# Conversions of later weight blocks queued behind the last routing, product groups placed between routing steps, and a second result buffer

## The chip, the cores and the metric

The kernel runs on one core of one Trainium2 chip. The metric is the time of one execution on the device in microseconds (us); the figure given for a kernel is the median of its runs. A profile is one more execution, with every instruction recorded.

A core has five engines, each with its own queue that is worked through in the order in which the program was written out: TensorE (PE in the profile, its weight loads are PEld), VectorE (DVE), ScalarE (ACT), GpSimd (POOL) and SyncE (SP), which here only starts transfers.

## The reference

Three stages follow one another.

```python
# 1. a linear attention with a complex decay, per batch and head
S_re, S_im = ar*S_re - ai*S_im + k v^T, ar*S_im + ai*S_re
y[t] = q[t] @ S_re
# 2. a mixture of 8 experts, one expert for each token
expert_idx = np.argmax(x @ w_gate, axis=1)
out[mask] = gate_w[mask] * (np.maximum(xe @ w1[e], 0) @ w2[e])
# 3. a dense part
h = (x @ w1) * (x @ w2) @ w3
return h @ w_out
```

There are 3072 tokens of 384 numbers; the inner width of the experts and of the dense part is 1024. The weights of the dense part come as 64-bit floating point numbers.

## The kernel before

**Folding.** `w3 @ w_out` does not depend on the tokens. The kernel computes this 1024 x 384 matrix once (class `Fuse`, L670), writes it to device memory as `wf`, and later needs one product per token instead of two. The matrix has eight row blocks `f` of 128. `Fuse.product` (L707) makes a block with 24 matmuls into one PSUM bank: eight column tiles `g`, three matmuls each (`mm3`, L349, a split into a high and a low part). It yields after every second `g`, so a product is issued in four groups of six matmuls. Then ACT copies the bank to a buffer `ws` (L722), and SP stores `ws` to `wf` (L723). In the trace the first six products are named `Wf`, the last two `wpo`.

**Conversions.** Each block needs its weights as a high and a low 32-bit part, `w3h` and `w3l`. `Fuse._singles` (L681) generates these steps through `halves` (L313): eight units for `w_out`, then two for each of the eight blocks, "half blocks" below. A unit is spread over three successive steps: a first stage on DVE (L336, L337, L339) on the raw numbers `fdr` that SP has loaded, a stage on ACT (L329, L330), a second stage on DVE (L322, L323, L324) that writes `w3h` and `w3l`. There are five raw buffers, and `ahead` asks for loads up to two units ahead of the one in hand. The blocks' results lie in four sets of buffers; block `f` takes the set of block `f - 4`, so its second stage must wait until product `f - 4` has read it.

**Routing.** `route` (L110) takes two finished token tiles: transposes on PE (L122, `rt`), a copy by ACT (`xt`, L124), logits on PE (L131, `rl`), a copy by ACT (`lg`, L132), a chain of small DVE steps (maximum `mx`, L137; `key`; `kx`; one-hot `oh`, L144), ranks on PE (L147 to L150, `rk`), three DVE steps to the positions `pi` (L152 to L156), and on POOL an indirect transfer per tile (L160) that scatters its rows to the buffers of the experts, `xs`.

**Experts.** `moe` (L442) loads an expert's 432 rows of `xs` as `xe` (L385), transposes them (L395, `px`), splits them into `xh` and `xl`, and runs eight steps per expert. A step is `hstep` (L399): nine matmuls `ph`, a relu by ACT (`hh`, L406), a remainder by DVE (`hl`, L407); and `ystep`, nine matmuls `py`. After each `hstep` the loop asks the generator of the products for one more piece (L492), so the last two products and their conversions come here, one piece per step; when they are used up, the conversion of the other dense weights begins (`moe2_weights`, L506).

**What sets the order.** The program is traced in the order of the Python code, and a scheduler then writes out a queue for each engine. It prefers what was traced earlier, but puts in later work where it reckons that an engine would stand idle. `tc.issue_after(ins)` adds a constraint: what is traced in that block stays behind `ins` on the engine of `ins`, and only on that engine. Before the change all conversions are held behind `S.end` alone (L702), the last DVE step of attention's keys, so those of blocks 4 to 7 may be put in anywhere after it. Four blocks are asked for during the last group of attention (L1132). The loop in `build` (L1332) then issues products until six blocks are done, all of it behind `x.lasty`, attention's last output matmul. The conversions of blocks 4 and 5 are traced in this loop, those of 6 and 7 in the expert steps.

Of the kernel before, what the change touches and what calls it, by code (L numbers as in the profile page):

```python
# [1 line left out]

# [6 lines left out]
F32 = mybir.dt.float32  # L9
# [11 lines left out]
DM = 384  # L21
KD = 3
NE = 8
FF = 1024
NF = 8
# [71 lines left out]
def bc(ap, n, at):  # L97
    shape = list(ap.shape)
    return ap.unsqueeze(at).to_broadcast(shape[:at] + [n] + shape[at:])
# [10 lines left out]
def route(tc, S, slot0, xtiles, bank=None):  # L110

    nc = tc.nc
    n = len(xtiles)
    sp = S.rpool
    bank = bank or (lambda name: S.rpsum.tile([128, 512], F32, tag="tr", name=name, bufs=2))
    slots = slice(slot0, slot0 + n)
    lg, mx = S.lg[:, slots], S.mx[:, slots]
    xts = []
    for i, x in enumerate(xtiles):
        pt = bank(f"rt{slot0}_{i}")[:, : KD * 128].rearrange("p (k c) -> p k c", k=KD)  # L120
        for k in range(KD):
            nc.tensor.transpose(pt[:, k], x[:, k * 128 : (k + 1) * 128], S.ident)  # L122
        xts.append(sp.tile([128, KD, 128], F32, tag="xt", name=f"xt{slot0}_{i}", bufs=2))
        nc.scalar.copy(xts[-1], pt)  # L124
        yield 330
        if i % 2:
            yield None
            pl = bank(f"rl{slot0}_{i}")
            for j, xt in enumerate(xts):
                for k in range(KD):  # L130
                    nc.tensor.matmul(pl[:, j * NE : (j + 1) * NE], xt[:, k], S.wg[:, k], start=(k == 0), stop=(k == KD - 1))  # L131
            S.logits = nc.scalar.copy(lg[:, i - 1 : i + 1].rearrange("p i e -> p (i e)"), pl[:, : 2 * NE])  # L132
            xts = []
            yield 1280
    t8 = lambda nm: sp.tile([128, n, NE], F32, tag=nm, name=f"{nm}{slot0}")
    v = nc.vector
    v.reduce_max(out=mx[:, :, 0], in_=lg, axis=AX.X)  # L137
    key = t8("key")
    for i in range(n):
        v.scalar_tensor_tensor(out=key[:, i], in0=lg[:, i], scalar=mx[:, i], in1=S.efirst, op0=ALU.is_ge, op1=ALU.mult)  # L140
    kx = sp.tile([128, n, 1], F32, tag="kx", name=f"kx{slot0}")
    v.reduce_max(out=kx[:, :, 0], in_=key, axis=AX.X)
    oh = t8("oh")
    v.tensor_tensor(out=oh, in0=key, in1=kx.to_broadcast([128, n, NE]), op=ALU.is_equal)  # L144
    yield None
    rk = bank(f"rk{slot0}")[:, : n * NE].rearrange("p (i e) -> p i e", e=NE)
    nc.tensor.matmul(rk, S.ones, bc(S.run, n, 1), start=True, stop=False)  # L147
    nc.tensor.matmul(rk, S.upper, oh, start=False, stop=n == 1)
    for i in range(1, n):
        nc.tensor.matmul(rk[:, i:], S.ones, bc(oh[:, i - 1], n - i, 1), start=False, stop=i == n - 1)  # L150
    r2 = t8("r2")
    v.tensor_tensor(out=r2, in0=rk, in1=oh, op=ALU.mult)  # L152
    pos = S.pos[:, slots]
    v.reduce_sum(out=pos, in_=r2, axis=AX.X)
    pi = sp.tile([128, n], I32, tag="pi", name=f"pi{slot0}")
    S.routed = v.tensor_copy(pi, pos)  # L156
    for i in range(n):
        v.tensor_tensor(out=S.run, in0=S.run, in1=oh[:, i], op=ALU.add)
    for i, x in enumerate(xtiles):
        S.scatter = nc.gpsimd.indirect_dma_start(  # L160
            out=S.xsv[slot0 + i], out_offset=bass.IndirectOffsetOnAxis(ap=pi[:, i : i + 1], axis=0),
            in_=x, in_offset=None, bounds_check=NE * CAPR - 1, oob_is_err=False,
        )
    yield 640
# [113 lines left out]
def ahead(load, srcs, n):  # L278

    got = []  # L280
    for i in range(len(srcs)):
        while len(got) < min(i + n, len(srcs)):
            got.append(load(srcs[len(got)]))
        yield got[i]
# [155 lines left out]


def moe(tc, S, fuse, product):  # L442

    nc = tc.nc
    extra = moe2_weights(tc, S)
    with ExitStack() as pools:
        pool = lambda n, bufs, **kw: pools.enter_context(tc.tile_pool(name=n, bufs=bufs, **kw))
        steps = [(e, j) for e in range(NE) for j in range(NF)]
        LA, LR = 1, 4
        x = Expert(tc, S, pool("mw", 3), None, None, S.rpsum, None)  # L450
        ws, xs, xraw = {}, {}, {}
        wraw = {i: x.load_w(*steps[i], nc.sync) for i in range(LR)}
        yield
        x.xp, x.hp, x.py = pool("mx", 2), pool("mh", 2), pool("mpy", 1, space=PSUM)
        fuse.psum = lambda f, name: x.py.tile([128, 512], F32, tag="px", name=name, bufs=KD)
        xraw[0] = x.load_x(0, nc.sync)
        def weights(i):
            with tc.issue_after(S.routed.ins), tc.issue_after(S.logits.ins):
                ws[i] = x.split_w(*wraw.pop(i))

        for i in range(LA):
            weights(i)
        xs[0] = x.make_xt(xraw[0])
        pend = None
        psy = None

        def flush():
            nonlocal psy
            i, h = pend
            e, j = steps[i]  # L470
            if j == 0:
                psy = x.py.tile([128, KD, 512], F32, tag="py", name="py")
            x.ystep(psy, h, ws[i], j)
            if j == NF - 1:
                x.store(psy, nc.scalar.value_load(S.offi[0:1, e : e + 1], min_val=0, max_val=NT))
            del ws[i]

        for i, (e, j) in enumerate(steps):
            if i + LR < len(steps):
                wraw[i + LR] = x.load_w(*steps[i + LR], nc.sync)  # L480
            if i + LA < len(steps):
                weights(i + LA)
            if j == 1 and e < NE - 1:
                with tc.issue_after(x.relu.ins):
                    xraw[e + 1] = x.load_x((e + 1) * CAPR, nc.scalar)
            h = x.hstep(xs[e], ws[i])
            if i == REND or (e, j) == (NE - 1, NF - 3):
                yield
            if pend is not None:
                flush()  # L490
            pend = (i, h)
            if next(product, None) is None:  # L492
                next(extra, None)
            if j == 5 and e + 1 < NE:
                with tc.issue_after(x.mark.ins):
                    xs[e + 1] = x.make_xt(xraw[e + 1])
            if j % 4 == 3 and i > NF:
                with tc.issue_after(x.late.ins):
                    next(S.places, None)
        flush()  # L500
        for x in (product, extra):
            for _ in x:
                pass
# [166 lines left out]
class Fuse:  # L670
# [10 lines left out]
    def _singles(self):  # L681
        nc, S, wp = self.nc, self.S, self.wp
        self.wo = [wp.tile([128, NF, DM], F32R, tag=f"wo{x}", name=f"wo{x}") for x in "hl"]
        self.w3 = []

        def factor(f):
            return lambda: [x[:, f] for x in self.wo]

        def block(f, h):
            def place():  # L690
                if not h:
                    pool = wp if f % W3B == 0 else self.w2p
                    self.w3.append([pool.tile([128, NF, 128], F32R, tag=f"w3{x}{f % W3B}", name=f"w3{x}{f}") for x in "hl"])
                return [x.rearrange("p g c -> p (g c)")[:, h * 512 : (h + 1) * 512] for x in self.w3[f]]
            return place

        srcs = [S.w_out[f * 128 : (f + 1) * 128, :] for f in range(NF)]
        srcs += [S.w3[f, :, h * 512 : (h + 1) * 512] for f in range(NF) for h in range(2)]
        raws = ahead(doubles(self.w2p, nc.sync, 5), srcs, 3)
        made = halves(S, nc, raws, wp, [factor(f) for f in range(NF)] + [block(f, h) for f in range(NF) for h in range(2)])  # L700
        for n in range(len(srcs) + 2):
            with self.tc.issue_after(S.end.ins):  # L702
                next(made)
            self.ready = max((n - 1 - NF) // 2, 0)
            yield

    def product(self):  # L707
        nc = self.nc
        for f in range(NF):
# [5 lines left out]
            for g in range(NF):  # L715
                mm3(nc, po[:, :DM], wh[:, g], wl[:, g], self.wo[0][:, g], self.wo[1][:, g], g == 0, g == NF - 1)
                if g % 2 and g < NF - 1:
                    if self.ready < min(f + W3B, BEFORE):
                        next(self.units)
                    yield 960  # L720
            ws = self.w2p.tile([128, DM], F32, tag="ws", name=f"ws_{f}")
            nc.scalar.copy(ws, po[:, :DM])  # L722
            nc.sync.dma_start(self.S.wf[f * 128 : (f + 1) * 128, :], ws)  # L723
            self.blocks = f + 1
# [558 lines left out]
BEFORE = 6  # L1283
W3B = 4


def build(ctx, tc, S):
    nc = tc.nc
# [7 lines left out]
    with ExitStack() as at:  # L1296
# [6 lines left out]
        x = Attn(tc, S, *(p.__enter__() for p in (qp, e2, ep)), st, pp, ap)  # L1303
# [25 lines left out]
            yield from x.groups(lambda *a: route(tc, S, *a), side, lambda: done)  # L1329

        drive([first(), second()])
        while side.fuse.blocks < BEFORE:  # L1332
            with tc.issue_after(x.lasty.ins):
                next(side.product)
    S.late = lambda name: ctx.enter_context(tc.tile_pool(name=name, bufs=1, side="right"))
    psum = tc.tile_pool(name="ph", bufs=2, space=PSUM)
# [59 lines left out]
```

## Time and profile before

| | |
|---|---|
| median of 3 runs | 1015.89 us (1015.53 to 1018.94) |
| the profiled execution, its own time | 1012.96 us |
| its span in the profile | 1011.2 us |
| PE busy | 896.7 us (89% of the span) |
| DVE busy | 610.1 us (60%) |
| ACT busy | 488.8 us (48%) |
| POOL busy | 126.8 us (13%) |

Times in the trace count from the start of the span. A matmul's start is its own; its end is modelled and overlaps the next one, so starts are compared below. A line of the timeline gives the start, the duration (of all instructions merged in it), the engine, the line, what it writes and reads, how many instructions are merged, and in brackets the idle time of the engine before it with what ended it. The granted clock of TensorE is given as a share of its full speed.

### The profile page before, as it was taken

What the parts mean: (1) busy time and instruction counts of PE and PEld (TensorE: products, weight loads), DVE (VectorE), ACT (ScalarE), POOL (GpSimd) and SP (SyncE); (2) the same over time, 40 slices, a digit from 0 to 9 for tenths busy, and PEclk for the clock granted to TensorE, in tenths of its full rate; (3) what the DMA queues carried; (4) which work ended last, traced back from release to release, by engine and by line L of the source; (5) the groups of instructions that cost most, each with busy time, mean ns of one, the idle gap of its engine ahead of it and who ended that gap; (6) DMA issues with size and microseconds to landing.
All of it is one profiled execution on the core that took longest, in us unless ns stands there. A gap on an engine that the chain in (4) does not pass through costs nothing. (4 is left out here: it accounts for less than half of the span.)

```text
span 1011.2 us, 17058 instructions
## 1 busy us (share of the span) xinstructions
PE 896.7 (89%) x6402; PEld 762.8 (75%) x6402; DVE 610.1 (60%) x1374; ACT 488.8 (48%) x1089; POOL 126.8 (13%) x197
## 2 busy tenths in 40 slices
PE   3544899968897899969989999998999999999997
PEld 1222478655786787969978999997888888888886
DVE  6899899797996797545379996443232323232222
ACT  6455588764874786424355665453222222121211
POOL 5111000102010101000222221110001010101011
PEclk9666899989998999979999999999999999999999
DMA  5556985339544973544585765550000000000000
GB/s 188 178 177 197 293 264 180 127 110 346 167 162 132 345 241 104 164 124 131 127 267 163 190 155 131 141 92 2 1 1 32 1 32 1 32 1 32 2 30 31
DMA packets 90183, 128.74 MB, mean 127 GB/s; under 512 B 7233, under 2 KB 72689, under 8 KB 90097
## 3 DMA queue, kind: packets, MB, share of 16 engines
q1 hardware_dynamic: 76300, 82.61, 29.0%
q0 software_dynamic: 10688, 40.36, 11.3%
q10 hardware_dynamic: 3108, 4.65, 1.8%
q8 instruction: 51, 0.84, 0.3%
q14 instruction: 36, 0.29, 0.1%
HBM read 92.38 MB, written 35.22 MB: 126 GB/s over the span
## 5 line engine op out<-in xcount | busy, mean ns | idle before, releaser
L605 DVE TENSOR_TENSOR ab<-asb,pb 128x512 f32<-128x512 f32 x48 | 33.0, 688 | 188.2 <-PE pb L352 184.9
L346 DVE TENSOR_TENSOR l<-w,h 128x384 fp32r<-128x384 f32 x128 | 70.8, 556 | 70.4 <-ACT h L345 64.3
L345 ACT CAST h<-w 128x384 fp32r<-128x384 f32 x128 | 65.4, 514 | 98.2 <-PE ph L351 50.5
L600 ACT COPY asb<-pa 128x512 f32<-128x512 f32 x48 | 28.2, 586 | 121.1 <-PE pa L352 117.2
L804 PE MATMUL x<-s,ident 128*128 128x384 f32 x64 | 35.6, 692 | 48.6 <-ACT s L856 48.4
L345 ACT CAST gh<-ab 128x512 fp32r<-128x512 f32 x48 | 29.8, 620 | 95.2 <-DVE ab L605 90.7
L351 PE MATMUL py<-hl,h 128*128 128x432 f32 x192 | 70.4, 367 | 2.9 <-DVE hl L407 2.8
L350 PE MATMUL py<-hh,h 128*128 128x432 f32 x192 | 69.7, 363 | 2.8 <-ACT hh L406 2.8
L350 PE MATMUL ph<-xh,h 128*128 128x432 f32 x192 | 69.9, 366 | 0.2 <-DVE hl L407 0.2
L352 PE MATMUL ph<-xh,l 128*128 128x432 f32 x192 | 69.6, 363 | 0.0
L351 PE MATMUL ph<-xl,h 128*128 128x432 f32 x192 | 69.4, 361 | 0.0
L352 PE MATMUL py<-hh,l 128*128 128x432 f32 x192 | 69.3, 361 | 0.0
L848 DVE TENSOR_TENSOR pr<-cf,P 128x192 f32<-128x192 f32 x189 | 66.7, 354 | 3.1
L351 PE MATMUL po<-ol,gh 128*128 128x384 f32 x192 | 64.9, 338 | 0.0
L350 PE MATMUL po<-oh,gh 128*128 128x384 f32 x192 | 64.8, 337 | 0.0
L352 PE MATMUL po<-oh,gl 128*128 128x384 f32 x192 | 64.0, 338 | 0.0
L961 PE MATMUL tr<-ident,kk 128*96 128x128 f32 x384 | 57.1, 281 | 6.9 <-DMA kk<-qkd 3.9
L804 PEld LDWEIGHTS x<-s,ident 128*128 128x128 f32 x64 | 15.0, 257 | 63.6 <-ACT s L856 54.6
L569 POOL DMA_INDIRECT out<-ob,mdp x24 | 23.8, 993 | 305.9 <-DVE ob L568 164.2
L962 ACT COPY qkT<-tr 96x512 f32<-96x512 f32 x96 | 53.3, 589 | 16.2 <-PE tr L961 12.9
L350 PE MATMUL pa<-yh,ah 128*128 128x512 f32 x144 | 57.0, 396 | 3.0 <-ACT yh L345 3.0
L351 PE MATMUL pb<-yl,bh 128*128 128x512 f32 x144 | 57.0, 396 | 0.0
(219 smaller groups left out, 2388.2 us busy)
## 6 DMA issues: line engine op xcount, KB each, us to landing
w<-in_w SPq DMA_DIRECT2D x128, 192.0 KB
kk<-qkd SPq DMA_DIRECT2D x24, 768.0 KB
qkd<-qk POOLq DMA_DIRECT2D x21, 768.0 KB
qkr<-in_qk SPq DMA_DIRECT2D x24, 384.0 KB
a<-in_a SPq DMA_DIRECT2D x11, 768.0 KB
fdr<-in_w SPq DMA_DIRECT2D x16, 512.0 KB
fdr<-in_v POOLq DMA_DIRECT2D x12, 512.0 KB
xs<-zr POOLq DMA_DIRECT2D x8, 648.0 KB
```

Source lines behind the costliest of these rows:

```text
L345: nc.scalar.copy(H, src)
L346: nc.vector.tensor_tensor(out=L, in0=src, in1=H.bitcast(F32), op=ALU.subtract)
L350: nc.tensor.matmul(out, lh, rh, start=first, stop=False)
L351: nc.tensor.matmul(out, lh, rl, start=False, stop=False)
L352: return nc.tensor.matmul(out, ll, rh, start=False, stop=last)
L569: nc.gpsimd.indirect_dma_start(out=S.outv[j], out_offset=bass.IndirectOffsetOnAxis(ap=S.mdp[:, j, 0:1], axis=0), in_=ob, in_offset=None, b ...
L600: nc.scalar.copy(asb, pa)
L605: nc.vector.tensor_tensor(out=ab, in0=asb, in1=pb, op=ALU.mult)
L804: nc.tensor.matmul(p, S.ident, s[r], start=r == 0, stop=r == 1)
L848: v.tensor_tensor(out=pr, in0=twice(cf[i][:, t]), in1=bc(pv, 2, 1), op=ALU.mult)
L961: nc.tensor.transpose(pt[:, h], qk[:, h0 + h, w], self.S.ident)
L962: nc.scalar.copy(qkT[:, w, h0 : h0 + 4], pt)
```

## The change

The conversions are cut in two lists: the eight units of `w_out` and those of blocks 0 to 3 stay behind `S.end`; those of blocks 4 to 7 go behind `S.gate`. In `route` this is set to `S.routed` (the copy to `pi`, on DVE) and `S.logits` (the copy to `lg`, on ACT); in the expert loop to the relu and the remainder of the step just traced. The pieces of the products in `build` go behind different PE instructions by their number: piece 0 behind `x.lasty`, 1 behind the last transposes, 2 and 3 behind the last logits, all later ones behind the last ranks. Loads of raw numbers are asked for one unit earlier. The buffer `ws` comes from two pools in turn.

```diff
@@ route
-            nc.tensor.transpose(pt[:, k], x[:, k * 128 : (k + 1) * 128], S.ident)
+            S.rt = nc.tensor.transpose(pt[:, k], x[:, k * 128 : (k + 1) * 128], S.ident)
...
-                    nc.tensor.matmul(pl[:, j * NE : (j + 1) * NE], xt[:, k], S.wg[:, k], start=(k == 0), stop=(k == KD - 1))
+                    S.rl = nc.tensor.matmul(pl[:, j * NE : (j + 1) * NE], xt[:, k], S.wg[:, k], start=(k == 0), stop=(k == KD - 1))
...
-        nc.tensor.matmul(rk[:, i:], S.ones, bc(oh[:, i - 1], n - i, 1), start=False, stop=i == n - 1)
+        S.rk = nc.tensor.matmul(rk[:, i:], S.ones, bc(oh[:, i - 1], n - i, 1), start=False, stop=i == n - 1)
...
     S.routed = v.tensor_copy(pi, pos)
+    S.gate = S.routed, S.logits
@@ moe
             h = x.hstep(xs[e], ws[i])
+            S.gate = x.relu, x.late
@@ Fuse._singles
-        raws = ahead(doubles(self.w2p, nc.sync, 5), srcs, 3)
-        made = halves(S, nc, raws, wp, [factor(f) for f in range(NF)] + [block(f, h) for f in range(NF) for h in range(2)])
-        for n in range(len(srcs) + 2):
-            with self.tc.issue_after(S.end.ins):
-                next(made)
+        raws = ahead(doubles(self.w2p, nc.sync, 5), srcs, 4)
+        first = [factor(f) for f in range(NF)] + [block(f, h) for f in range(W3B) for h in range(2)]
+        rest = [block(f, h) for f in range(W3B, NF) for h in range(2)]
+        for n, _ in enumerate(self._bound(halves(S, nc, raws, wp, first), lambda: [S.end])):
             self.ready = max((n - 1 - NF) // 2, 0)
+            yield
+        for n, _ in enumerate(self._bound(halves(S, nc, raws, wp, rest), lambda: S.gate)):
+            self.ready = W3B + max((n - 1) // 2, 0)
+            yield
+
+    def _bound(self, steps, behind):
+        while True:
+            with ExitStack() as order:
+                for x in behind():
+                    order.enter_context(self.tc.issue_after(x.ins))
+                if next(steps, self) is self:
+                    return
             yield
@@ Fuse.product
-            ws = self.w2p.tile([128, DM], F32, tag="ws", name=f"ws_{f}")
+            ws = (self.wp if f % 2 else self.w2p).tile([128, DM], F32, tag="ws", name=f"ws_{f}")
@@ build
-        while side.fuse.blocks < BEFORE:
-            with tc.issue_after(x.lasty.ins):
+        for n in count():
+            if side.fuse.blocks >= BEFORE:
+                break
+            with tc.issue_after((x.lasty, S.rt, S.rl, S.rl, S.rk)[min(n, 4)].ins):
                 next(side.product)
```

## Rows read from the trace of the kernel before

**Rows 1.** Stretches: busy us (instructions) of PE, PEld, DVE, ACT, POOL; PE clock; DMA share, GB/s.

```profile
400.00:420.00 20.00, 19.16 (x203) 18.06 (x204) 7.96 (x19) 7.55 (x16) 1.94 (x2) 1.00 0.50 162
...
435.00:440.00 5.00, 0.87 (x5) 0.55 (x4) 2.71 (x6) 0.48 (x1) 0.00 (x0) 0.80 0.82 263
440.00:445.00 5.00, 1.18 (x7) 1.21 (x8) 0.00 (x0) 0.14 (x1) 0.00 (x0) 0.50 0.48 164
445.00:450.00 5.00, 5.00 (x23) 4.80 (x22) 1.82 (x3) 1.42 (x3) 0.00 (x0) 0.67 0.00 0
...
460.00:480.00 20.00, 20.00 (x111) 19.18 (x110) 11.49 (x27) 8.71 (x18) 0.00 (x0) 1.00 0.36 105
480.00:500.00 20.00, 20.00 (x105) 19.27 (x104) 7.41 (x15) 8.81 (x19) 2.14 (x2) 1.00 0.48 129
```

**Rows 2.** Waits of PE from 444 us on: total us, times, longest us.

```profile
PE px L395 <- DMA xe<-xs: 8.0, 1, 8.0
...
PE py L351 <- DVE hl L407: 2.8, 3, 1.2
```

**Rows 3.** Timeline of PE from attention's end to the first expert steps.

```profile
406.79 0.44 PE L350 MATMUL Wf<-woh,w3h 128*128 128x384 f32 x1
...
415.44 0.81 PE L131 MATMUL rl<-wg,xt 128*128 128x8 f32 x6
...
426.77 0.44 PE L350 MATMUL Wf<-woh,w3h 128*128 128x384 f32 x1 [1.20 <-ACT ws L722]
...
429.16 0.29 PE L148 MATMUL rk<-oh,upper 128*128 128x16 f32 x2
...
435.53 0.34 PE L352 MATMUL Wf<-woh,w3l 128*128 128x384 f32 x1
443.82 2.39 PE L395 MATMUL px<-ident,xe 108*128 108x108 f32 x12 [7.95 <-DMA xe<-xs]
445.90 1.07 PE L350 MATMUL ph<-xh,h 128*128 128x432 f32 x2
...
448.20 0.37 PE L350 MATMUL wpo<-woh,w3h 128*128 128x384 f32 x1
```

**Rows 4.** Timelines of ACT, DVE, POOL and SP: the last routing and the load of its tokens.

```profile
417.91 0.14 ACT L132 COPY lg<-rl 128x16 f32<-128x16 f32 x1
...
426.36 0.17 DVE L144 TENSOR_TENSOR oh<-key,kx 128x16 f32<-128x16 f32 x1
...
431.39 0.16 DVE L156 CAST pi<-pos 128x2 int32<-128x2 f32 x1
...
433.64 1.10 POOL L160 DMA_INDIRECT xs<-xo,pi  x1 [0.30 <-issue]
...
438.63 0.37 SPq L385 DMA_DIRECT2D xe<-xs  x1
```

**Rows 5.** Timelines of ACT and DVE: the routing just before the last one.

```profile
396.75 0.17 ACT L132 COPY lg<-rl 128x16 f32<-128x16 f32 x1
...
399.61 0.17 DVE L144 TENSOR_TENSOR oh<-key,kx 128x16 f32<-128x16 f32 x1
...
402.44 0.17 DVE L156 CAST pi<-pos 128x2 int32<-128x2 f32 x1
```

**Rows 6.** Conversions: three lines of DVE's timeline, then groups from 406.8 to 446 us.

```profile
393.44 0.69 DVE L324 SCALAR_TENSOR_TENSOR w3l<-fdr,fdm 128x512 fp32r<-128x512 f32 x1
...
412.00 1.29 DVE L322 TENSOR_TENSOR w3h<-fdr,fdm 128x512 fp32r<-128x512 f32 x2 [9.38 <-PE Wf L351]
...
413.88 1.29 DVE L324 SCALAR_TENSOR_TENSOR w3l<-fdr,fdm 128x512 fp32r<-128x512 f32 x2
...
L722 ACT COPY ws<-Wf 128x384 f32<-128x384 f32 x6 | 2.8, 473 | 6.9 <-DMA wf<-ws 6.8
L336 DVE TENSOR_SCALAR fdm<-fdr 128x512 int32<-128x512 int32 x6 | 2.4, 421 | 0.0
L339 DVE SCALAR_TENSOR_TENSOR fdr<-fdr,fdl 128x512 f32<-128x512 uint32 x3 | 2.1, 685 | 0.0
```

More of the change, by code (lines that the diff above doesn't have):

```diff
@@ L1 @@
 from contextlib import ExitStack, nullcontext
+from itertools import count
 import concourse.bass as bass
```

## The prediction

> **What bounds the kernel now.** I read the busy time by stretches first. TensorE (PE) is nearly full from 400 us on except in one place: in 435 to 445 us it works 2 of 10 us, and its granted clock is down to 0.50, the lower of its two levels (1.2 GHz) [rows 1]. The table of waits names the cause: one wait of 8.0 us, the transposes `px` of the first expert's tokens for the load `xe` of those tokens [rows 2]. It is the longest of PE's waits from 444 us to the end. In the timeline, the last product of the folded weights ends at 435.53 + 0.34 = 435.87, `px` starts at 443.82, the first expert matmul `ph` at 445.90 [rows 3]. Until the next product's matmul at 448.20 the expert matmuls are slow: a mean clock of 0.67 over 445 to 450 means 3.3 of these 5 us at half, so up to 448.3 [rows 1, 3].
>
> Why is `xe` late? Followed back [rows 4]: `xe` is issued at 438.63, 5.0 us after the last scatter of routed tokens starts (433.64); the scatter follows the positions `pi` (431.39); these follow the one-hot `oh` (426.36) and the logits `lg` (417.91). Attention's last output matmuls are over when the first product starts, 406.79 [rows 3]. So the last routing takes 25 us. It shares three queues with less urgent work. On PE its logits stand between matmuls of products 0 and 1 (the last six start at 415.44, its ranks at 429.16) [rows 3]. On VectorE (DVE) conversions of blocks 4 to 7 lie between its small steps; one of block 4 held the queue 9.38 us because product 0 still read the buffer that it overwrites [rows 6]. The pair routed just before went from `lg` (396.75) to `pi` (402.44) in 5.7 us, with a few conversion steps between [rows 5], against 13.5 us for the last one.
>
> **The change, part by part.** *Order on PE.* A product is 24 matmuls, four groups of six. Now group 0 goes behind attention's last matmul, group 1 behind the last transposes, groups 2 and 3 behind the last logits, everything else behind the last ranks. A group costs at most 1.16 us: 27.9 us of PE from 406.79 to 435.87 without its 1.20 us wait, over 24 groups, with the routing's own matmuls in it [rows 3]. The last transposes then start at 408.0; 0.5 for them (three matmuls; six of the logits took 0.81), 1.16 for group 1 (which hides the copy of the transposed tokens) and 0.8 for the logits give 410.4. From `lg` to the end of `oh` the pair before took 3.0 us [rows 5]. The handover before `lg` lies between 0 and the last routing's 1.66 us (416.25 to 417.91) [rows 3, 4]; I take 0.35, since the conversions on ACT that lay there are held back too. The ranks can start at 413.8. Groups 2 and 3 cover PE to 412.7, so PE idles 0 to 2.4 us here; I take 0.5, since conversion steps lay in that 3.0 us as well. From the end of `oh` to the end of `pi` it took 2.8 us there (399.78 to 402.61): `pi` at about 416, the second scatter at 417.5, `xe` 5.0 later at 422.5, landed 5.2 later (438.63 to 443.82) at 428 [rows 3 to 5]. The products last to 435.87 - 1.20 + 0.5 = 435.2. So the load has 7 us to spare and the 8 us wait is gone.
>
> *Two result buffers.* The copy of a product out of PSUM waited for the store of the one before, 6.9 us in all, and PE for that copy once, 1.20 us [rows 3, 6]. With two buffers that wait has nothing left to wait for: the 1.20 us taken off above. Bounds 0 (another holder of the bank) and 1.2; I take 1.2.
>
> *Conversions of blocks 4 and 5, behind the last `pi` and `lg`.* All conversions of blocks 0 to 3 are done before the last routing (the last step of block 3 starts at 393.44) [rows 6], so nothing of them is left to disturb it. A half block costs DVE 1.59 us for its second stage (412.00 to 415.17 for two) and 1.53 us for its first (two of 0.42 and one of 0.69), 3.1 in all [rows 6]. Block 5 is ready after four halves and one first stage more, 14.0 us after `pi`: 430. Product 5 starts 4.6 us before the products' end, at 430.6. Margin 0.6 us; the splits of expert weights and small routing sums on DVE can eat it. Cost 0 to 3 us; I take 0, because the scheduler puts the earlier-traced conversions first.
>
> *Conversions of blocks 6 and 7, now behind expert steps.* Before, they filled DVE while PE waited. Now four second stages and two first ones, 4 x 1.59 + 2 x 1.53 = 9.4 us, run beside expert matmuls. DVE is busy there only 18.9 of 40 us while PE is full [rows 1]: 21 us are free, so on average it fits, but a unit behind one step's `hl` can delay the next. Between 0 (all covered) and 9.4 (nothing covered) I take 1.0, near the covered end. If that cover fails, PE waits for `hl`. Products 6 and 7 also no longer fill PE around the first expert steps; I count nothing beyond this 1.0.
>
> *Loads.* One more raw load is asked for ahead; on SP's queue the last of them waits for block 5's first second stage (near 423) and could hold `xe` behind it until then, still 7 us early. POOL's queue gets nothing new; its two scatters only come earlier. Cost 0, covered by the same slack.
>
> *Sum.* `px` waits for the last product's copy out of PSUM, 0.47 us [rows 6], 0.8 with its handovers, and `px` to `ph` took 2.08 us at the low clock [rows 3]; at the high one it lies between half of that and all of it; I take 1.7, since copies by ACT and DVE are most of it. New `ph` at 435.2 + 0.8 + 1.7 = 437.7. The old one at 445.90 with 2.4 us at half clock behind it stands for 447.1 at full clock. Gain 9.4, less 1.0: **8.4 us**. PE is full in the stretches that follow [rows 1], so the shift should reach the end. The profiled execution took 1012.96, so 1004.6; the median of the runs is 1015.89, 2.9 above it, which gives **1007.5**.
>
> A rule against it: short gaps. The new order puts several short waits between PE's groups, where the old one ran 20 us almost unbroken. What the rows show is a clock of 1.00 over 400 to 420 us, with attention's short waits in it [rows 1], and a fall only around the 8 us wait. The Trainium skill ("TensorE: Matmul & The Clock Gate", section "A second HAM failure mode: psum-queue depth-cycling") says that frequent micro-idling between groups of matmuls makes the clock swing to its lower level. By that rule a further low stretch would come; the trace of before doesn't bear it out for gaps of about 1 us. As a mechanism here it is rival 3.
>
> **The rivals.** *1. Late expert steps.* The conversions of blocks 6 and 7 are not covered: each `hl` of the first steps stands behind them. For: they come in bunches, DVE has its own work in every step, and PE did wait for `hl` later on, where DVE was loaded (2.8 us in three waits) [rows 2]. Against: the 21 us free. Price up to 9.4 instead of 1.0, so a gain of 0 to 5; time about 1012 to 1016. Chance 0.11.
> *2. Late block 5.* The margin of 0.6 us fails and PE waits 2 to 3 us for product 5's weights; gain about 6, time 1010. Chance 0.07.
> *3. Low clock among the products.* One more stretch at 0.50 as long as the one seen (from 438.0 to 448.3, 10.3 us) [rows 1] loses half of it, 5.2 us, leaving 3.2: 1012.7. Chance 0.03.
> *4. Slower: the ranks as a gate.* Every group but four stands behind the ranks. From the last six logits matmuls to the ranks it was 13.7 us in this trace (415.44 to 429.16) [rows 3]. If that stays, because something else sits in DVE's or ScalarE's (ACT) queue, groups 2 and 3 cover 2.3 us and logits 0.8, PE idles 10.6, and then works at the low clock for some 4.5 us more (443.82 to 448.3), losing 2.3. `ph` comes at 437.7 - 0.5 + 10.6 + 2.3 = 450.1, against 447.1: 3.0 slower, plus 1.0 to 9.4 from the conversions: 1020 to 1028. It decides from about 9 us of idling. Against: what filled those 13.7 us are the conversions that now go behind. Chance 0.05.
> *5. No effect.* The gain is given back at PE's later waits for `hl` [rows 2], or the orders change little. The PE edges cannot be missed, so only the first counts. About 1015. Chance 0.04.
>
> **How the numbers follow.** The forecast holds 0.70: gains from 6 to 13 us (8.4 with up to 2 us more where `px` slips in ahead of product 5, up to 1.5 for conversion steps that leave attention's end, the 1.0 at 0; down by 2 for small waits). No change that a measurement can tell is 0.5%, 5.1 us: faster means under 1010.8, slower over 1021. Faster: the forecast, rival 2 and a tenth of rival 1, 0.78. Slower: 0.05, from rival 4. Same: 0.17. The range, 1001.5 to 1013.0, takes in the forecast, rivals 2 and 3 and the nearer part of rival 1.
>
> **What would show it.** Right: no wait of `px` for `xe`; last transposes near 408, ranks near 413, scatters before 420; no conversion of blocks 4 to 7 between `lg` and `pi`; clock 1.00 from 400 to 500; first `ph` between 436 and 439; all conversions of blocks 6 and 7 behind the first `hl`. Wrong: ranks later than 418, a new wait of product 5 for `w3h` or `w3l`, `py` waiting for `hl` for more than 3 us in the first twelve expert steps, or a first `ph` that is early with an end that is not.

## The result and the profile after

The changed kernel takes 1005.27 us (median of 6 runs, 1001.68 to 1006.9) against 1017.38 (6 runs, 1008.33 to 1019.63) for the kernel before beside it: a ratio of 0.9882 [0.9849, 0.9914], 9 to 15 us less. That is faster by more than 0.5%, inside the forecast range and 2.2 us below its number. The profiled execution took 1003.89 us (span 1002.1) against 1012.96: 9.1 us less, where 8.4 were forecast.

Executions differ in when they reach the first product's matmul: 408.08 us here, 406.79 before. So below, places count from that matmul ("+29.5"), and **the stretch** is the time from it to the dense part's first matmul `pa`: 295.8 us before, 285.5 after, 10.35 less. The first `ph` comes at +29.5 instead of +39.1, which is 9.65; the expert steps from `ph` to `pa` take 256.0 instead of 256.7. At `pa` itself PE waits 3.02 us for `yh`, the converted input of the dense part, in every kernel alike. Of the kernel before there is one profile, so a difference to it carries the spread of single executions.

PE's timeline of the changed kernel (all its line numbers are new: `px` is L397, `ph` L352, `hl` L409):

```profile
408.08 0.44 PE L352 MATMUL Wf<-woh,w3h 128*128 128x384 f32 x1
...
411.36 0.81 PE L132 MATMUL rl<-wg,xt 128*128 128x8 f32 x6
...
414.23 0.29 PE L149 MATMUL rk<-oh,upper 128*128 128x16 f32 x2
...
435.33 0.34 PE L354 MATMUL Wf<-woh,w3l 128*128 128x384 f32 x1
436.28 1.33 PE L397 MATMUL px<-ident,xe 108*128 108x108 f32 x12 [0.61 <-ACT ws L736]
437.54 0.66 PE L352 MATMUL ph<-xh,h 128*128 128x432 f32 x2
...
442.02 0.46 PE L352 MATMUL py<-hh,h 128*128 128x432 f32 x1 [0.45 <-ACT hh L408]
...
497.33 0.46 PE L353 MATMUL py<-hl,h 128*128 128x432 f32 x1 [1.04 <-DVE hl L409]
```

Against [rows 3]: the ranks start 6.2 us behind the first product, not 22.4, with groups 2 and 3 ending just ahead of them. The products run without a bracket to 435.67, `px` waits 0.61 us for the last copy, and no longer 7.95 for `xe`. New is the wait at 442 us for the first `hh` (0.45, and 0.22 for the first `hl` behind it); waits like the one at 497 us the kernel before had too, from 509 us on.

The last routing on the other engines, from the timelines of ACT, DVE, POOL and SP:

```profile
412.21 0.17 ACT L133 COPY lg<-rl 128x16 f32<-128x16 f32 x1 [1.33 <-PE rl L132]
...
413.37 0.18 DVE L145 TENSOR_TENSOR oh<-key,kx 128x16 f32<-128x16 f32 x1
...
415.18 0.17 DVE L157 CAST pi<-pos 128x2 int32<-128x2 f32 x1
415.26 0.42 DVE L338 TENSOR_SCALAR fdm<-fdr 128x512 int32<-128x512 int32 x1
...
431.79 0.68 DVE L326 SCALAR_TENSOR_TENSOR w3l<-fdr,fdm 128x512 fp32r<-128x512 f32 x1
...
442.56 0.68 DVE L324 TENSOR_TENSOR w3h<-fdr,fdm 128x512 fp32r<-128x512 f32 x1
...
417.50 1.10 POOL L162 DMA_INDIRECT xs<-xo,pi  x1 [0.30 <-issue]
...
422.76 0.37 SPq L387 DMA_DIRECT2D xe<-xs  x1
```

From `lg` to `pi` it takes 3.0 us where it took 13.5 [rows 4]; the conversion of block 4 starts right behind `pi`, the last half of block 5 is done at 431.79 + 0.68, and the second stages of block 6 come behind the first `hl`, from 442.56. `xe` is issued 14.7 us behind the first product instead of 31.8.

The stretches in which the clock was low before [rows 1] (busy us and instructions of PE, PEld, DVE, ACT, POOL; PE clock; DMA share, GB/s):

```profile
435.00:440.00 5.00, 4.39 (x27) 3.54 (x27) 1.64 (x3) 1.84 (x4) 0.00 (x0) 1.00 0.11 39
440.00:445.00 5.00, 4.33 (x22) 3.56 (x21) 3.43 (x8) 3.44 (x7) 0.00 (x0) 1.00 0.35 105
445.00:450.00 5.00, 5.00 (x29) 4.86 (x28) 5.00 (x13) 2.45 (x5) 0.00 (x0) 1.00 0.54 162
```

PE works 8.7 us of 435 to 445 instead of 2.1, at a clock of 1.00. One short low stretch comes later, in the expert steps, and the kernel before has one like it there (0.86 over 530 to 535, 0.80 over 535 to 540). After:

```profile
520.00:525.00 5.00, 2.14 (x10) 1.45 (x9) 4.47 (x10) 3.72 (x9) 1.17 (x2) 1.00 0.63 192
525.00:530.00 5.00, 5.00 (x19) 4.67 (x18) 5.00 (x12) 3.17 (x8) 2.71 (x3) 0.66 0.76 242
```

A mean of 0.66 over 5 us is 3.4 us at half, which costs 1.7 us. PE's waits from the first product to 690 us (total us, times, longest us):

```profile
PE py L353 <- DVE hl L409: 3.9, 4, 1.8
...
PE py L352 <- ACT hh L408: 2.5, 2, 2.1
PE px L397 <- ACT ws L736: 0.6, 1, 0.6
```

The 8.0 us of [rows 2] are gone. The wait for `hl` is 3.9 us instead of 2.8.

### The profile page after: what moved, and what is told of

Its sections match the earlier page's. It is cut to its first block, busy times and chain, and to the rows that moved or that the text cites. A ratio compares the mean times of both kernels' runs of the same rounds, so it can differ in the third digit from the quotient of the medians.

```text
span 1002.1 us, 17063 instructions
## 1 busy us (share of the span) xinstructions
PE 898.0 (90%) x6402; PEld 764.9 (76%) x6402; DVE 609.6 (61%) x1374; ACT 488.5 (49%) x1089; POOL 130.3 (13%) x197
## 3 DMA queue, kind: packets, MB, share of 16 engines
q1 hardware_dynamic: 76300, 82.61, 29.1%
## 5 line engine op out<-in xcount | busy, mean ns | idle before, releaser
L352 PE MATMUL py<-hh,h 128*128 128x432 f32 x192 | 69.3, 361 | 2.5 <-ACT hh L408 2.5
L352 PE MATMUL ph<-xh,h 128*128 128x432 f32 x192 | 69.6, 363 | 0.0
L352 PE MATMUL po<-oh,gh 128*128 128x384 f32 x192 | 64.8, 337 | 0.0
L352 PE MATMUL pa<-yh,ah 128*128 128x512 f32 x144 | 57.1, 396 | 3.0 <-ACT yh L347 3.0
```

The source lines that it names most:

```text
L352: nc.tensor.matmul(out, lh, rh, start=first, stop=False)
```

## The experiments

Eleven runs were made in three groups, each group beside runs of the kernel before; a0 and a1 are the changed kernel again, e10 is e4 again. For each stands the ratio to the kernel before with its interval, and from one profile the places at which the products end and `ph` starts, the stretch, and the time from `ph` to `pa`. The last column is that time less half of what was spent in it at the low clock: the expert steps at full clock.

| kernel | ratio | products end | `ph` | stretch | `ph` to `pa` | at full clock |
|---|---|---|---|---|---|---|
| before | 1 | +29.1 | +39.1 | 295.8 | 256.7 | 253.8 |
| changed | 0.9882 [0.9849, 0.9914] | +27.6 | +29.5 | 285.5 | 256.0 | 254.3 |
| changed (a0) | 0.9843 [0.9799, 0.9886] | +27.6 | +29.5 | 284.1 | 254.7 | 254.7 |
| changed (a1) | 0.9875 [0.9838, 0.9911] | +27.6 | +29.5 | 283.2 | 253.8 | 253.8 |
| e1 order only | 0.9965 [0.9932, 0.9998] | +34.0 | +35.8 | 290.9 | 255.0 | 251.6 |
| e2 gate only | 0.9894 [0.9845, 0.9943] | +34.0 | +36.6 | 296.1 | 259.5 | 255.6 |
| e3 one buffer | 0.9876 [0.983, 0.9922] | +27.6 | +29.5 | 283.9 | 254.5 | 252.8 |
| e4 no step gate | 0.9792 [0.9743, 0.984] | +27.6 | +29.5 | 280.0 | 250.5 | 250.5 |
| e10 no step gate | 0.9849 [0.9814, 0.9884] | +27.6 | +29.5 | 281.2 | 251.7 | 250.0 |
| e5 load behind store 3 | one run | +27.6 | +29.5 | 282.4 | 252.9 | 252.9 |
| e6 load behind store 5 | one run | +27.6 | +35.8 | 290.3 | 254.6 | 251.9 |
| e7 no step gate, new weights later | 0.9788 [0.9754, 0.9822] | +27.6 | +29.4 | 279.4 | 250.0 | 250.0 |
| e9 step gate, new weights later | 0.9859 [0.9825, 0.9893] | +27.6 | +29.5 | 282.1 | 252.6 | 250.6 |

**The order on PE alone (e1).** The conversions of blocks 4 to 7 stay free behind `S.end`, with one `ws` and the loads as before:

```diff
-        for n, _ in enumerate(self._bound(halves(S, nc, raws, wp, rest), lambda: S.gate)):
+        for n, _ in enumerate(self._bound(halves(S, nc, raws, wp, rest), lambda: [S.end])):
-            ws = (self.wp if f % 2 else self.w2p).tile(...)
+            ws = self.w2p.tile(...)
-        raws = ahead(..., srcs, 4)
+        raws = ahead(..., srcs, 3)
```

> Only the order on TensorE is changed; conversions, loads and result buffer as before. Measure: the stretch from the first product matmul to the first matmul of the dense part, 295.8 us before, 285.5 after, and inside it the issue of the first tokens' load, 31.8 us after the first product matmul before, 14.7 after. Theory A (the tokens' load was late because the routing was late; any way of having it before the products end is enough): the positions come some 3 to 6 us later than in the changed kernel, since a conversion still stands ahead of them on VectorE, the load starts 17 to 22 us after the first product matmul, the transposes do not wait for it, and the stretch is 285 to 288 us; time 0.988 to 0.993 of before. Theory B (the gate on the conversions is what freed the routing): the ranks wait behind conversions, TensorE idles ahead of them, the load is issued later than 26 us, and the stretch stays above 291 us; time above 0.995.

The load is issued at +20.6, 11 us earlier than before, and its wait is gone; but the products end at +34.0, 6.4 later than with the whole change. From the timelines of SP, ACT and PE of this kernel:

```profile
431.72 0.37 SPq L387 DMA_DIRECT2D xe<-xs  x1
432.19 0.35 SPq L737 DMA_DIRECT2D wf<-ws  x1
...
437.78 0.48 ACT L736 COPY ws<-Wf 128x384 f32<-128x384 f32 x1 [4.99 <-DMA wf<-ws]
...
438.31 0.69 PE L352 MATMUL Wf<-woh,w3h 128*128 128x384 f32 x1 [3.76 <-ACT ws L736]
```

Read upwards: PE waits 3.76 us for the copy of a product, the copy waits 4.99 us for the buffer, and the store that frees it is written behind `xe` on SP's queue, which itself had to wait for the scatters. The clock then falls (435 to 440 us, same columns as above):

```profile
435.00:440.00 5.00, 1.69 (x5) 1.69 (x6) 1.13 (x3) 0.48 (x1) 0.00 (x0) 0.67 0.67 243
```

So the order alone removes one wait and makes another out of the same load, half as long. It keeps 4.95 us of the 10.35 in the stretch, 3.3 of them at `ph`. The load was issued when theory A said, but the stretch and the time are not A's, and B's late load did not come either: neither theory had the store. A second result buffer, which this kernel leaves out, was not tried with it.

**The gate alone (e2).** The pieces of the products stay behind `x.lasty`, as before:

```diff
-        for n in count():
-            if side.fuse.blocks >= BEFORE:
-                break
-            with tc.issue_after((x.lasty, S.rt, S.rl, S.rl, S.rk)[min(n, 4)].ins):
+        while side.fuse.blocks < BEFORE:
+            with tc.issue_after(x.lasty.ins):
                 next(side.product)
```

and `ws` and `raws` as in e1.

> Only the conversions of later blocks are held behind the last routing and behind expert steps; product order, loads and result buffer as before. Theory A: the ranks still stand behind half of the products on TensorE, so the load starts 22 to 27 us after the first product matmul and lands at 27 to 33 us, about when the products end (28 us); the transposes wait 0 to 3 us for it, the stretch is 286 to 290 us, time 0.988 to 0.995 of before. Theory C (both parts are needed, neither does it alone): load later than 28 us, wait of 5 us or more, stretch above 292 us, time above 0.995.

PE's timeline:

```profile
422.57 0.29 PE L149 MATMUL rk<-oh,upper 128*128 128x16 f32 x2
...
429.04 0.44 PE L352 MATMUL Wf<-woh,w3h 128*128 128x384 f32 x1 [1.49 <-DVE w3h L324]
...
430.92 0.69 PE L354 MATMUL Wf<-woh,w3l 128*128 128x384 f32 x1 [1.26 <-DVE w3l L326]
...
440.30 0.44 PE L354 MATMUL Wf<-woh,w3l 128*128 128x384 f32 x1 [1.06 <-DVE w3l L326]
...
443.60 0.59 PE L397 MATMUL px<-ident,xe 108*128 108x108 f32 x4 [1.29 <-ACT ws L736]
```

The logits again stand among the products, the ranks come at +14.3, `pi` at +15.2. Now the conversions wait for `pi`, and PE waits for them: 1.49, 1.26 and 1.06 us for `w3h` and `w3l`. It is rival 2, with the gate late instead of the chain of conversions. The load is issued at +22.4, and `px` does not wait for it. The clock falls here too:

```profile
430.00:435.00 5.00, 4.08 (x16) 4.09 (x17) 5.00 (x12) 1.35 (x4) 0.00 (x0) 0.66 0.63 193
```

The times say that this kernel gains (0.9894), its one profile that the stretch gains nothing (296.1); but the profiled execution, 1017.3 us, was the longest of its four runs (median 1011.57). What the gate alone is worth stays open; that its products end 6.4 us later than with both parts is in the rows. The load was as early as theory A said, and the stretch as long as theory C said, for a reason that neither gave.

**One result buffer (e3).**

```diff
-            ws = (self.wp if f % 2 else self.w2p).tile(...)
+            ws = self.w2p.tile(...)
```

> The changed kernel with one result buffer. Theory A: the second buffer is worth the wait that TensorE had for the copy, 0 to 1.5 us; the stretch is 285.5 to 287 us, time within 0.3% of the changed kernel (0.987 to 0.992 of before). Rival D (the stores were what blocked): TensorE waits for copies several times, 4 us or more in all, stretch above 289 us.

Nothing is lost: products' end, `ph` and the ratio agree with the changed kernel. ACT's copy still waits for the store, 7.4 us in three times, but among the products PE never waits for the copy. **The buffer was worth nothing here; the 1.20 us that I credited to it [rows 3] went with the rest of the change.** Why the store was late before can be read from the timelines of ACT and SP and from SP's waits of the kernel before:

```profile
420.45 0.47 ACT L722 COPY ws<-Wf 128x384 f32<-128x384 f32 x1
...
421.80 0.33 SPq L291 DMA_DIRECT2D fdr<-in_w  x1
422.22 0.38 SPq L723 DMA_DIRECT2D wf<-ws  x1
...
426.24 0.48 ACT L722 COPY ws<-Wf 128x384 f32<-128x384 f32 x1 [1.62 <-DMA wf<-ws]
```

```profile
SPq L291 <- DVE w3l L324: 7.7, 2, 6.2
```

The copy of product 1 was done at 420.92, but its store went out at 422.22. Ahead of it on SP's queue stood a load of raw numbers, which had waited 6.2 us for DVE to free its buffer. These 1.3 us are about what PE then waited (1.20). In e3 the same store goes out 0.5 us behind the start of its copy, and the raw loads come later.

**No gate on the steps (e4, and again as e10).**

```diff
             h = x.hstep(xs[e], ws[i])
-            S.gate = x.relu, x.late
```

> The changed kernel, but the conversions of the last two blocks are held behind the last routing alone and not behind expert steps. Theory A with the step gate as a small cost: conversions of the last two blocks move ahead, VectorE is free in the first expert steps, the 0.7 us that TensorE waits there for the first relu and remainder goes, and products again fill in; the stretch is 284 to 286 us. Rival E (the step gate protects the first expert steps): the first splits of expert tokens or the first remainders stand behind conversions, TensorE waits 2 us or more there, stretch above 287.5 us.

> The changed kernel without the step gate, again, now beside the changed kernel. If the step gate's removal gains: stretch from the first expert matmul to the dense part 249.5 to 252 us, waits for relu and remainder 2 to 4 us, and a time 3 to 6 us under the changed kernel's. If the first look was a lucky execution: stretch 253.5 us or more and a time within 2 us of the changed kernel's.

PE's waits from 430 us on, first in the changed kernel (its run a1), then in e10:

```profile
PE py L353 <- DVE hl L409: 3.6, 4, 1.8
...
PE py L352 <- ACT hh L408: 2.0, 2, 1.6
```

```profile
PE py L353 <- DVE hl L409: 1.6, 2, 0.8
PE py L352 <- ACT hh L408: 1.2, 1, 1.2
```

At full clock the expert steps take 250.5 and 250.0 us without the gate; with it 253.8 to 254.7 in the changed kernel's three profiles, and 251.9 to 252.9 in e3, e5 and e6, which have the gate too. The two groups don't overlap; the gate costs 1.4 to 4.7 us, in the mean 3.1 (253.4 against 250.3). In the times it is not shown: beside each other e10 took 1002.68 us and a1 1004.39, 1.7 less where 3 to 6 were expected, with intervals that overlap.

Rival E is out: the gate protects nothing. Without it PE does not wait for `hh` or `hl` in the first expert steps, only 0.18 us for `xl` in e10; with it PE waits 0.44 and 0.21 us there, at +33.9 and +34.6. The stretches, 280.0 and 281.2 us, are shorter than the 284 to 286 of theory A. The rest of the cost lies mainly at +89 to +98, where the next experiments look.

**The load later (e5, e6).** SP's load of `xe` is written behind the store of product 3, or 5:

```diff
-        xraw[0] = x.load_x(0, nc.sync)
+        with tc.issue_after(fuse.stored[3].ins):
+            xraw[0] = x.load_x(0, nc.sync)
...
```

> The changed kernel with the load of the first tokens held on SyncE's queue behind the store of the fourth product. Theory A (any arrival before the products end is enough; slack of about 8 us): the load is issued some 20 us after the first product matmul, not 14.7, lands near 25.5, the transposes do not wait for it, and the first expert matmul still comes at 29.5 us. Rival F (the earlier start of the load is itself worth something, or something else waits for it): the first expert matmul comes 2 us or more later.

> The changed kernel with that load held behind the store of the sixth product. Theory A: issued near 28.6 us after the first product matmul, landed 5.2 us later, so the transposes wait 5 to 6.5 us, the clock falls to its lower level, the first expert matmul comes at 35 to 37 us, and the stretch to the dense part is longer by the same 6 to 8 us: the wait is paid in full. Rival G (the wait is given back later): the first expert matmul is as late, but the stretch to the dense part grows by less than 3 us.

In e5 the load is issued at +20.5, 5.8 us later than in the changed kernel, and `ph` stays at +29.5: slack. In e6 it is issued at +28.8. From SP's and PE's timelines of e6:

```profile
438.42 0.38 SPq L387 DMA_DIRECT2D xe<-xs  x1
...
443.31 2.39 PE L397 MATMUL px<-ident,xe 108*128 108x108 f32 x12 [6.11 <-DMA xe<-xs]
445.39 1.07 PE L352 MATMUL ph<-xh,h 128*128 128x432 f32 x2
```

```profile
440.00:445.00 5.00, 1.69 (x10) 1.72 (x11) 0.09 (x1) 0.52 (x1) 0.00 (x0) 0.56 0.36 125
```

A wait of 6.1 us for `xe`, 2.08 us instead of 1.26 from `px` to `ph`, and the low clock are back; `ph` is 6.3 us later, and the stretch is 6.2 longer than in a0 beside it. This is the most direct evidence for the main step: with all else as in the changed kernel, a late load alone costs 6.3 us at `ph`. Against the three profiles of the changed kernel the stretch is 4.9 to 7.1 us longer, so within that spread the wait is paid in full.

**The changed kernel again, and the new weights later (a0, a1, e7, e9).** The waits for `hl` and `hh` remained. DVE's timeline in the changed kernel showed what stood ahead of the `hl` that PE waited for at 497.33:

```profile
495.27 0.43 DVE L306 TENSOR_SCALAR fda<-fdr 128x512 int32<-128x512 int32 x1 [4.68 <-DMA fdr<-in_v]
...
496.68 0.60 DVE L409 SCALAR_TENSOR_TENSOR hl<-ph,hh 128x432 fp32r<-128x432 f32 x1
```

The first conversion of the next stage's dense weights had come to the head of DVE's queue before its raw numbers had landed, and held the queue 4.68 us. So in e7 and e9 these loads are asked for two expert steps before the first conversion and their pieces go behind each step's relu and remainder; e7 leaves out the step gate of the blocks, e9 keeps it:

```diff
-                next(extra, None)
+                with tc.issue_after(x.relu.ins), tc.issue_after(x.late.ins):
+                    next(extra, None)
...
+        raws = chain([next(raws)], raws)
+        for _ in range(2):
+            yield
         plain = ahead(part, ..., 2)
```

> The changed kernel once more, beside the others on this chip. From the first product matmul to the first expert matmul 29.5 us as in its profile; to the first matmul of the dense part 284 to 287 us, where the spread comes from the waits around the conversion of the other dense weights; time 0.985 to 0.991 of before.

> Without the step gate, and with the conversion of the other dense weights begun two expert steps after its loads are issued, each piece behind the relu and the remainder of the step at hand; an attempt at a version better than both. Theory H (the waits for remainders around 90 to 115 us after the first product matmul come from conversions that stand on VectorE's queue ahead of a remainder while their load is still under way): TensorE's waits for relu and remainder between the first expert matmul and the dense part fall from 3 to 6 us to under 2 us, that stretch of 250.5 us (without step gate) shrinks to 247 to 249.5 us; time 0.974 to 0.980 of before. Rival I (the waits are VectorE's load, not its order): waits of 3 us or more, stretch 250 us or more.

> The changed kernel beside the next two on one chip, with more rounds. From the first expert matmul to the dense part 254 to 256.5 us, waits for relu and remainder there 4 to 7 us; time 0.984 to 0.990 of before.

> The step gate kept, the conversion of the other dense weights begun two expert steps after their loads. Theory J (the step gate costs little itself, 0.5 to 1 us in the first expert steps; most of what was lost with it lay in the order of VectorE's queue around the other weights): the waits after 80 us from the first product matmul fall under 2.5 us, the stretch from the first expert matmul to the dense part is 250 to 252 us, time 0.976 to 0.984 of before. Theory K (the step gate itself costs the 4 to 5 us): that stretch stays at 253.5 us or more, time 0.983 or more.

PE's waits from 430 us on, in e7:

```profile
PE py L353 <- DVE hl L409: 2.0, 3, 0.8
...
PE py L352 <- ACT hh L408: 0.2, 1, 0.2
```

DVE's wait for `fdr` is gone in both, and the expert steps take 250.0 us in e7 and 250.6 in e9 at full clock. So late weights bring little where there is no gate (e7 against 250.5 and 250.0 in e4 and e10), short of theory H's 247 to 249.5. With the gate they take away all but 0.6 us of its cost, which is the two waits of 0.44 and 0.21 us in the first steps; e9 has no other wait for `hh` or `hl` up to +155. That is theory J's mechanism, from one profile each. In the times it is not shown: e9 took 1002.91 us, a ratio of 0.9859 where J expected 0.976 to 0.984.

It is not that the conversions of the last blocks, held back by the gate, run into those of the next stage. DVE's timelines, first the end of the last block's conversions in the changed kernel, then the hold in e10:

```profile
472.60 0.69 DVE L326 SCALAR_TENSOR_TENSOR w3l<-fdr,fdm 128x512 fp32r<-128x512 f32 x1
```

```profile
498.87 0.43 DVE L306 TENSOR_SCALAR fda<-fdr 128x512 int32<-128x512 int32 x1 [2.48 <-DMA fdr<-in_v]
```

The last blocks are done at +65.2, some 17 us before the first new conversion comes to the head of the queue. What differs is how long that one holds it: 4.4 to 5.1 us in the three profiles of the changed kernel, 2.4 and 2.5 in e4 and e10. With the gate the last product is copied 1.1 us later (+79.8 instead of +78.8), and the loads of the new weights are issued 0.55 us behind that copy in all five profiles. That they also take 6.5 to 7.2 us from issue to first use, instead of 4.5 and 4.6, stays unexplained.

In the times e7 is the fastest of all, 999.23 us beside 1004.17 for a0 in the same group; the ratios' intervals just overlap. The changed kernel's own repeats lie at the edge of what was expected of them: a0's ratio 0.9843 (0.985 to 0.991), a1's steps 253.8 us (254 to 256.5).

## Why the prediction was right, and where it was not

- **The bound was read right.** The wait for `xe` and the low clock behind it were the loss, both are gone, and e6 brings them back by the load's date alone.
- **Order on PE.** Forecast for the ranks, `pi`, the second scatter and `xe`, as distances from the first product: +7.0, 9.2, 10.7 and 15.7. Measured: 6.2, 7.1, 9.4 and 14.7. From `lg` to `pi` it took 3.0 us instead of the 5.7 of the pair before [rows 5], for no conversion step stands in the chain now. That takes both parts: in e1 (order only) conversions stand in it and it takes 5.8, in e2 (gate only) the ranks stand behind products on PE and it takes 5.8 too. PE did not idle ahead of the ranks; I had taken 0.5. Rival 4, the ranks as a gate, needed 9 us of idling there.
- **Two parts that need each other.** I had written of the order and the gate as separate items, and credited the early positions to both. e1 and e2 show more: either alone brings the load early enough, and either alone, tried with one result buffer and the loads as before, ends the products 6.4 us later than the whole change. The gate without the order makes block 4 late; the order without the gate leaves a store behind the load. The loads asked for one unit earlier were never tried by themselves.
- **The second buffer was the step that failed.** "With two buffers that wait has nothing left to wait for": true, but with one buffer PE does not wait either (e3). The term of 1.2 us came out right by luck, since the wait did go; its cause was misread. I took one row with ACT's copy as the holder and did not ask why the store was late: it stood behind a load of raw numbers on SP's queue, and that load behind DVE. That a second buffer would help in e1's order is argued, not tried.
- **Block 5.** Ready 17.3 us behind `pi` where I had 14.0: the splits of expert weights that I had named as a risk stand between, 2.9 us. As distances from the first product that is +24.4 instead of +23.2, and product 5 begins at +23.4, so my margin of 0.6 us was a lack of 1.0. It cost nothing, because the last half block is read only by the second half of that product's 4.2 us, from +25.5. The term of 0 was right for a reason that I had not given, which is luck.
- **The sum at `ph`.** I made the old `ph` 30.9 + 9.4 = 40.3 us behind the first product at full clock, the new one 30.9. It came at 29.46, 1.4 earlier: 0.8 from the products' end (27.6 instead of 28.4), 0.2 from the wait of `px`, 0.4 from `px` to `ph` (1.26 instead of 1.7).
- **Expert steps.** I took 1.0 us off for conversions behind them. Against before, the changed kernel lost 0.4 at full clock (a mean of 254.25 against 253.82), which is less than the 0.9 by which its three profiles differ. It is a difference of two larger things: the gate costs some 3 us, as e4 and e10 show, and the kernel before had like waits, 2.8 and 2.8 us for `hl` and `hh`. Of the gate's cost only the 0.66 us in the first steps lies where I had placed it; the longer hold of DVE at the new weights was not in my sum.
- **Rival 3** did not come among the products, where it was placed: the clock is 1.00 from 400 to 450 us. In the expert steps it did fall for 3.4 us behind waits of 2.05 and 0.81 us, at a price of 1.7 us. The kernel before has such a fall too, behind waits of 1.76 and 1.23 us near 532, which my "a fall only around the 8 us wait" had left out. The Trainium skill ("TensorE: Matmul & The Clock Gate", section "A second HAM failure mode: psum-queue depth-cycling") says that frequent micro-idling between groups brings the low level. These falls fit it, but the size of the waits does not say when one comes: pairs of 1.22 and 0.82 us (e10) and of 1.17 and 0.61 (e9) were followed by 3.4 us at the low level, pairs of 1.86 and 0.80 (a0), 1.60 and 0.81 (a1) and 1.48 and 0.81 (e4) by none.
- **The size.** Between medians the gain was 12.1 us, between the two profiled executions 9.1, forecast 8.4. In the stretch it is 10.35, and 11.55 against the mean of the changed kernel's three profiles. Of the 10.35, 9.65 is the earlier `ph`, the rest the expert steps, at whose start the clock is no longer low. The 1.95 above the forecast are the 1.4 at `ph` and about half of the 1.0 taken off.

## What to carry to other kernels

When a late transfer stalls the busiest engine, follow it back through every queue that its inputs share, and move the whole chain: the urgent steps forward on one engine and the bulk work behind them on the others; one half of such a change can make a new wait of the same load. Try a constraint that is meant as protection without it: the gate on the expert steps protected nothing, and cost where the next stage's loads came. Before crediting a buffer with a wait, ask why the transfer that frees it is late.

## What was not expected

- The same program reaches its first product at 405.24, 408.08 and 410.73 us in three executions (a0, changed, a1), 5.5 us apart, while from there to `ph` they agree to 0.01 us. From `ph` to `pa` they differ again, by 2.3 us. Parts worth 1 to 4 us drown in the times of whole runs; a stretch between two fixed instructions shows them where its own spread is small.
- Two executions of one kernel had nearly the same two waits (2.05 and 0.81 us, 1.86 and 0.80), and the clock fell behind one pair alone. PE's timeline in the changed kernel:

```profile
522.77 0.47 PE L352 MATMUL py<-hh,h 128*128 128x432 f32 x1 [2.05 <-ACT hh L408]
524.04 0.47 PE L353 MATMUL py<-hl,h 128*128 128x432 f32 x1 [0.81 <-DVE hl L409]
...
525.41 0.56 PE L353 MATMUL py<-hl,h 128*128 128x432 f32 x1
```

  and in a0, where the matmuls that follow stay at 0.35:

```profile
520.13 0.47 PE L352 MATMUL py<-hh,h 128*128 128x432 f32 x1 [1.86 <-ACT hh L408]
521.40 0.46 PE L353 MATMUL py<-hl,h 128*128 128x432 f32 x1 [0.80 <-DVE hl L409]
```

- One conversion whose raw numbers are late holds DVE for 4.68 us. PE waits 1.04 us for the `hl` behind it, and 1.84 for another 9 us later; e9, where nothing holds DVE there, has neither wait. The loss is smaller than the hold, and it is not all paid at once.
- Where no edit holds it back, the load of `xe` is issued 4.5 to 5.9 us behind the start of the last scatter (5.0 before, 5.3 after), and is used 4.9 us behind its own issue where PE waits for it (e6): about 10 us for a round trip through device memory that no engine's busy time shows.
